# Moving the token-order copies, the SyncE order and the storing of results in a fused attention and MLP kernel

## The chip, the cores and the metric

The kernel runs on one core of a Trainium2 chip. The metric is the device time of one execution in microseconds (us). A core has five engines with instruction streams of their own: TensorE (PE in the profile; its weight loads are PEld), VectorE (DVE), ScalarE (ACT), GpSimd (POOL) and SyncE (SP). SyncE and GpSimd also issue the DMA transfers here; all transfers share the core's 16 DMA engines. An engine takes its instructions in order, and so do the two issuers: an instruction that waits holds up all that stand behind it.

## The reference

There are two stages. The first is attention over 8 batch rows (B), 8 heads (H), 576 positions (S) and a head size (D) of 64. Heads 0 to 3 are sliding: a query sees itself and the 31 positions before it. Heads 4 to 7 are dilated: a query sees every fourth position among the last 128.

```python
mask_plain = (rel >= 0) & (rel < window)                                     # window = 32
mask_dil = (rel >= 0) & (rel < window * dilation) & (rel % dilation == 0)    # dilation = 4
scores = np.where(masks[None, :, :, :], scale * q @ k.T, -1e9)
attn = np.exp(scores - max); attn = attn / (attn.sum(-1) + 1e-9)
x = (attn @ v).transpose(0, 2, 1, 3).reshape(B * S, H * D)                   # 4608 x 512
h = x @ w_in; r = np.maximum(h, 0.0); out = (r * r) @ w_out                  # 512 -> 2048 -> 512
```

(The middle lines are shortened; the meaning is that of the reference.) The second stage is a two-layer network with a squared ReLU between the layers. Inputs and output are fp32.

## The kernel before

**Tiling.** The attention works on one batch row (576 tokens) at a time; the network works on nine chunks of 512 tokens. While PE computes the attention of row b it also computes chunk b-1. The chunk is a Python generator that yields after every few matmuls; `pump(n)` takes n such steps. The attention's program calls `pump` between its own pieces, and so the order of PE's instructions is written out by hand: there is no planner (`tc.manual_schedule()`). Rows 2 to 7 are in a loop at the end of the function; rows 0 and 1 stand in front of it.

**A row.** `attn_scores` computes the scores of the sliding heads (`s_sliding`, tile ps) and of the dilated heads (`s_dilated`, tile pz). ACT takes the exponential into AT, and DVE multiplies AT by the mask. `attn_values` or, from row 4, `attn_values_by_dma` multiplies by the values (`av_sliding`, tile pav, three times with index mp; `av_dilated`, tile paw, four times). DVE normalizes each (`normalize`: a reciprocal and a multiplication, lines 594 and 599). ps, pz, pav and paw share one pool of two PSUM buffers (tag "pa"), so a buffer is free only once DVE or ACT has read it. Then x is transposed into xT, the input of the network: by PE (tiles px and py, copied by ACT) in rows 0 to 3, by DMA transposes in rows 4 to 7 (`x_sliding_by_dma` straight into xT; `x_dilated_by_dma` into yd, from which ACT copies, `x_from`).

**What a row needs of the next one.** q and k have to be transposed into QKTp (sliding) and QKTd (dilated). For rows 2 to 7 this goes through DRAM:

- sliding: GpSimd loads q and k into SBUF (`load_sliding_qk`, tile ns), an engine copies them into token order (`by_token`, line 120, tile nr; DVE, but GpSimd for row 2), SyncE stores them to DRAM (`keep_sliding_qk`, tile dp, line 217), and SyncE transposes them from there (`transpose_sliding`, line 225);
- dilated: GpSimd copies from DRAM to DRAM (`keep_dilated_qk`, tile dd), and SyncE transposes (`transpose_dilated`, line 229).

The values v are loaded by SyncE (sv and sd, lines 132 and 137) and cast by GpSimd into vp and vd. Each block of values also needs a "halo", the end of the block before it on other partitions: ACT copies it in rows 0 and 1 (`halo_sliding`, `halo_dilated`, lines 184 and 189), SyncE copies it by DMA in rows 2 to 7 (lines 194 and 197).

**Order on GpSimd.** `after_transposes(b)` is a tiny GpSimd copy that reads the row's last transposed tile. GpSimd waits there until the transposes have landed, and asks for the next row's q and k only then.

**The copy's place.** In the loop the copy (`turn`) is called from `attn_scores`, hook 3: behind the last dilated scores, in front of the first `normalize` of the values. On DVE it stands there in the program.

**The network.** `mm1_gen` computes one chunk's h (tile ph); ACT applies the ReLU (rt), DVE squares (g). Chunks 0 and 1 use an ordinary second layer (tile po, `store` copies to tile ot and issues a DMA for each 128 tokens). Chunks 2 to 8 use one level of Strassen's scheme (`mm2_strassen_gen`, tiles pa, pb, pc), whose DVE sums gs and g come at the end of mm1. Its results are ou and ov, 512 KB each, and SyncE issues their stores (`leave`) as soon as they are done. ot, ou and ov share a pool of three buffers (`otp`).

## Time and profile before

| | us |
|---|---|
| median of 8 runs | 310.32 (307.46 to 311.36) |
| the profiled execution | 311.36 |
| its span in the trace | 309.1 |

| engine | busy us | share of the span |
|---|---|---|
| PE | 288.3 | 93% |
| DVE | 209.0 | 68% |
| PEld | 192.9 | 62% |
| ACT | 170.8 | 55% |
| POOL | 67.2 | 22% |

The granted clock of TensorE was 1.0. The kernel moved 47.25 MB by DMA, 153 GB/s on the mean; in the slices from about 8 to 230 us the DMA engines are mostly 70 to 100% busy, after that hardly. PE starts at 5.2 us and has short tasks up to 26 us; row 1 runs from about 40 us, row 2 from 62, row 3 from 97, row 4 from 129, row 5 from 161, row 6 from 192 and row 7 from 222 us; chunks 7 and 8 alone take 252.6 to 304.7 us.

How to read it: a row of the timeline gives the start and the length in us, the engine, the line of the kernel, the operation and its tiles, the number of instructions merged into it and, in brackets, how long the engine had been idle before and what released it. Rows of SPq and of DMA operations give the time of issuing, not of the transfer; the landing comes some us later.

### The profile page before, as it was taken

The page shows a single profiled execution, that of the slowest core. Times are in us where ns is not written, and L with a number is a line of the kernel's source. Part 1 is how long each engine was busy: PE and PEld are TensorE (multiplying, and loading weights), DVE is VectorE, ACT ScalarE, POOL GpSimd, SP SyncE. Part 2 cuts the span into 40 slices and gives each one's busy share as a digit, 9 for nine tenths or more (in the row PEclk, how much of TensorE's full clock was granted, in tenths as well). Part 3 has the DMA queues.
Part 4 walks back from the last instruction along what each step waited for, and adds up shares of the span by engine and source line. Part 5 has one row for each costly group of instructions (what it writes and reads, how often), then busy time and mean ns, then how long its engine had stood idle before and what let it go on. Part 6 is the DMA issues. An engine that isn't in the chain of part 4 may idle for free.

```text
span 309.1 us, 6889 instructions
## 1 busy us (share of the span) xinstructions
PE 288.3 (93%) x2762; PEld 192.9 (62%) x2762; DVE 209.0 (68%) x433; ACT 170.8 (55%) x288; POOL 67.2 (22%) x117
## 2 busy tenths in 40 slices
PE   0998998999899999997999999989999999999994
PEld 0644554554455558753898998548855875785583
DVE  7685448668953698477948893989389934834652
ACT  1765648667525863494349535953496446425620
POOL 4381008412805301330035003500240000000000
PEclk9999999999999999999999999999999999999999
DMA  7799996899899999998979998999862130003004
GB/s 113 160 207 215 206 192 109 171 224 219 131 214 210 215 184 196 172 233 187 163 157 257 206 161 159 258 204 154 161 182 40 27 116 33 2 1 138 0 0 138
DMA packets 77521, 47.25 MB, mean 153 GB/s; under 512 B 58545, under 2 KB 69297, under 8 KB 77489
## 3 DMA queue, kind: packets, MB, share of 16 engines
q1 hardware_dynamic: 68416, 32.13, 49.7%
q0 software_dynamic: 9072, 14.68, 27.1%
q8 instruction: 21, 0.34, 0.5%
q14 instruction: 12, 0.09, 0.1%
HBM read 36.70 MB, written 16.52 MB: 172 GB/s over the span
## 4 chain that ended last, share of the span: by engine, by line
PE 68%; DMA 18%; DVE 4%; SPq 3%; POOL 2%; ACT 2%; issue 2%; POOLq 0%
PE ph L299 25%; PE pa L376 15%; DMA ns<-in_q_dram 9%; PE po L442 8%; PE pb L376 7%; DMA QKTd<-dd 4%; PE pc L376 4%; PE paw L627 3%; DMA sv<-in_v_dram 2%; DMA vd<-vd 2%; PE pf L496 2%; PE pav L611 2%; DMA vp<-vp 1%; SPq L229 1%; SPq L225 1%
## 5 line engine op out<-in xcount | busy, mean ns | idle before, releaser
L299 PE MATMUL ph<-xT,wi 128*128 128x512 f16 (+1 forms) x640 | 134.0, 359 | 0.7 <-ACT xT L664 0.7
L322 ACT ACTIVATE rt<-ph 128x512 f16<-128x512 f32 x144 | 86.2, 611 | 48.6 <-PE ph L299 41.2
L299 PEld LDWEIGHTS <-wi 128*128 128x128 f16 x640 | 68.2, 114 | 46.1 <-issue 0.6
L323 DVE TENSOR_TENSOR g<-rt 128x512 f16<-128x512 f16 x144 | 62.8, 448 | 36.9 <-ACT rt L322 36.0
L376 PEld LDWEIGHTS <-g 128*128 128x128 f16 x448 | 43.3, 98 | 6.1
L376 PEld LDWEIGHTS <-gs 128*128 128x128 f16 x336 | 31.9, 98 | 4.4 <-DVE gs L333 0.8
L442 PE MATMUL po<-wo,g 128*128 128x512 f16 x128 | 33.1, 379 | 0.0
L403 DVE TENSOR_TENSOR ov<-pb,ov 128x512 f32<-128x512 f32 x14 | 9.7, 692 | 30.7 <-PE pb L376 17.3
L376 PE MATMUL pa<-wt,gs 128*128 128x256 f16 x224 | 27.5, 273 | 0.0
L376 PE MATMUL pb<-wt,g 128*128 128x256 f16 x224 | 27.1, 273 | 0.0
L169 POOL CAST vp<-sv 128x512 f16<-128x512 f32 x24 | 14.4, 630 | 51.8 <-DMA sv<-in_v_dram 51.8
L177 POOL CAST vd<-sd 128x512 f16<-128x512 f32 (+1 forms) x32 | 22.5, 731 | 9.7 <-PE ps L562 5.4
L392 ACT COPY ov<-pa 128x512 f32<-128x512 f32 x14 | 8.2, 586 | 27.0 <-PE pa L376 27.0
L553 DVE TENSOR_TENSOR AT<-AT,maskp 128x576 f16<-128x576 f16 x32 | 19.2, 619 | 5.1 <-ACT AT L552 4.0
L599 DVE TENSOR_TENSOR xd<-paw,rcp_d 80x512 f16<-80x512 f32 (+1 forms) x32 | 21.9, 684 | 1.1
L552 ACT ACTIVATE AT<-pz 128x576 f16<-128x576 f32 x32 | 19.9, 707 | 1.9 <-PE pz L581 1.8
L552 ACT ACTIVATE AT<-ps 128x576 f16<-128x576 f32 x32 | 19.2, 659 | 1.6 <-PE ps L562 1.1
L611 PEld LDWEIGHTS <-AT 128*128 128x128 f16 x192 | 9.2, 99 | 12.9 <-issue 8.6
L599 DVE TENSOR_TENSOR xs<-pav,rcp_p 96x512 f16<-96x512 f32 x24 | 16.5, 686 | 0.8
L392 ACT COPY ou<-pa 128x512 f32<-128x512 f32 x14 | 8.2, 586 | 15.6 <-PE pa L376 15.6
L611 PE MATMUL pav<-vp,AT 128*128 128x65 f16 x192 | 10.5, 195 | 6.2 <-DVE xs L599 4.2
L553 DVE TENSOR_TENSOR AT<-AT,maskd 128x576 f16<-128x576 f16 x32 | 14.9, 496 | 1.2 <-ACT AT L552 0.4
(83 smaller groups left out, 279.5 us busy)
## 6 DMA issues: line engine op xcount, KB each, us to landing
sv<-in_v_dram SPq DMA_DIRECT2D x14, 288.0 KB, 5.6
dp<-nr SPq DMA_DIRECT2D x12, 288.0 KB, 4.1
out_dram<-ou SPq DMA_DIRECT2D x6, 512.0 KB, 4.0
out_dram<-ov SPq DMA_DIRECT2D x6, 512.0 KB, 4.9
sd<-in_v_dram SPq DMA_DIRECT2D x8, 320.0 KB, 5.8
ns<-in_k_dram POOLq DMA_DIRECT2D x8, 288.0 KB, 7.1
ns<-in_q_dram POOLq DMA_DIRECT2D x8, 288.0 KB, 8.1
sd<-in_v_dram SPq DMA_DIRECT2D x8, 256.0 KB, 6.3
```

The costliest lines, as they stand in the source:

```text
L169: nc.gpsimd.tensor_copy(vp[b % 2][:, m : m + 2, :, 0:D], sv[:, :, m : m + 2, :].rearrange("p h m d -> p m h d"))
L177: nc.gpsimd.tensor_copy(vd[b % 2][p0:P, t, c : c + 2, :, 0:D], sd[p0:P, t, :, D * c : D * (c + 2)].rearrange("p h (c d) -> p c h d", d=D),)
L299: nc.tensor.matmul(ph[:, t0:t1], wi4[ffc // 4][:, dmk, :, ffc % 4], xT[:, dmk, x0 : x0 + t1 - t0], start=(dmk == 0 and t0 == 0), stop=(dmk ...
L322: nc.scalar.activation(rt, ph[:], ACTF.Relu)
L323: nc.vector.tensor_mul(g[:, ffc, :], rt, rt)
L376: nc.tensor.matmul(banks[bank][:, t], a(k, t), b(k), start=(new and t == 0 and k == 0), stop=(k == HF - 1), skip_group_check=True,)
L392: nc.scalar.copy(ot, banks[A])
L442: nc.tensor.matmul(po, g[:, ffc, t * P : (t + 1) * P], wo[ffc // 4][:, ffc % 4, :], start=(ffc == 0), stop=(ffc == NFF - 1),)
L552: nc.scalar.activation(AT[:, u, 0:UW], ps[:, :, 0 : UW // 2], ACTF.Exp, scale=scale)
L553: nc.vector.tensor_mul(AT[:, u, 0:UW], AT[:, u, 0:UW], mask)
L599: nc.vector.tensor_tensor(out=x, in0=pv, in1=rb, op=ALU.mult)
L611: nc.tensor.matmul(pav[:, i, h * (D + 2) : h * (D + 2) + D + 1], AT[:, 2 * (h // 2) + m // 3, off : off + P], vp[b % 2][:, m, h, 0 : D + 1 ...
```

## The change

The change reorders work; matmuls, transfers of q, k and v, and the arithmetic stay.

1. The token-order copy of row 2 moves from GpSimd to DVE, and into row 1's values, behind the first dilated ones. For rows 3, 4 and 5 it moves from hook 3 of the scores to behind the second sliding values (mp == 1). For rows 6 and 7 it stays at hook 3.
2. `leave_half` can hold a store: it is put into the list `held`, and `leave_held()` issues it later. Held are the second half of chunks 0 and 1 and all of chunks 2 to 4. They are issued in the next row right behind the stores of the token-order copy (chunk 0's: behind row 2's transposes). Chunks 0 and 1 are stored by SyncE in two DMAs of 512 KB each, where there were four of 256 KB, chunk 0's by GpSimd.
3. Row 2's q and k are asked for before `cast_dilated_v(1)`. Its sliding transposes stand in front of the dilated ones, and `after_transposes(2)` reads QKTd like that of the other rows.
4. On SyncE, in rows 2 and 3: copy stores, held results, sv, sliding transposes, the dilated transpose of k, the vp halo, the dilated transpose of q, sd. From row 4 on: copy stores, held results, sliding transposes, sv, x, dilated x, dilated transposes, the vp halo, sd.
5. Row 2's halos are made by ACT. Row 1's first ACT halo goes behind its second sliding scores. The loop is split in two (rows 2 and 3, rows 4 to 7), with pumps of 22 and 14 instead of 24 and 16, and a gap of 4 instead of 3 in row 3's scores.

```diff
-        (nc.gpsimd if b == 2 else nc.vector).tensor_copy(
+        nc.vector.tensor_copy(
...
     def after_transposes(b):
-        t = QKTp[b % 2][:, 0, 1, PADP : PADP + 1] if b == 2 else QKTd[b % 2][:, 0, 1, KPAD : KPAD + 1]
-        nc.gpsimd.tensor_copy(seen, t)
+        nc.gpsimd.tensor_copy(seen, QKTd[b % 2][:, 0, 1, KPAD : KPAD + 1])
...
+    held = []
+    def leave_half(c, i, o, m, hold):
+        def go():
+            t0 = c * TOKC + HTOK * i
+            nc.sync.dma_start(
+                out=out[t0 : t0 + HTOK, m].rearrange("(t p) m -> p t m", p=P), in_=o[:, :, m]
+            )
+        if hold:
+            held.append(go)
+        else:
+            go()
+    def leave_held():
+        while held:
+            held.pop(0)()
...
         def leave(o, i, js):
+            leave_half(c, i, o, slice(HM * js[0], HM * (js[-1] + 1)), 1 < c < 5)
...
-        (nc.sync if c else nc.gpsimd).dma_start(out=out[(c * 4 + t) * P : (c * 4 + t + 1) * P, :], in_=ot)
+        if t % 2:
+            leave_half(c, t // 2, halves[c], slice(0, DM), t > 1)
...
+    ns = load_sliding_qk(2)
     cast_dilated_v(1)
-    ns = load_sliding_qk(2)
     dd = keep_dilated_qk(2)
-    nr = by_token(2, ns)
...
-    attn_scores(1, 2, 1)
-    attn_values(1, 1, True)
+    attn_scores(1, 2, 1, {1: lambda: halo_sliding(1, 0)})
+    dp = []
+    attn_values(1, 1, True, lambda: dp.append(keep_sliding_qk(2, by_token(2, ns))))
     pump(1000)
-    dp = keep_sliding_qk(2, nr)
+    transpose_sliding(2, dp[0])
     transpose_dilated(2, dd)
-    transpose_sliding(2, dp)
+    leave_held()
     load_v(2)
...
+        def turn_and_load():                       # rows 2 and 3, behind av_sliding mp == 1
+            dp = turn(nxt, ns)
+            leave_held()
+            load_sliding_v(nxt)
+            transpose_sliding(nxt, dp)
+            cast_sliding_v(nxt)
+            transpose_dilated(nxt, dd, (1,))
+            halo_sliding_by_dma(nxt)
+            transpose_dilated(nxt, dd, (0,))
+            load_dilated_v(nxt, nc.sync)
+        pump(22 if b == 2 else 14)
+        attn_scores(b, 4)
+        attn_values(b, b, False, turn_and_load)
...
+        def copied():                              # rows 4 to 6
+            if nxt < B:
+                dp = turn(nxt, ns)
+                leave_held()
+                transpose_sliding(nxt, dp)
+                load_sliding_v(nxt)
+        def loaded(y):
+            if nxt < B:
+                nc.gpsimd.tensor_copy(seen, y[:, 0, 0, 0:1])
+                cast_sliding_v(nxt)
+                transpose_dilated(nxt, dd)
+                halo_sliding_by_dma(nxt)
+                load_dilated_v(nxt, nc.sync)
+        pump(3)
+        attn_scores(b, 3, 0, {3: copied} if b > 4 else {})
+        attn_values_by_dma(b, copied if b == 4 else None, loaded)
```

(The two comments are added here; `turn` stores the copy that `by_token` makes.)

## The prediction, made before the result was known

> **What bounds the kernel now.** I read the page's busy shares and slices first (PE 288.3 of 309.1 us, granted clock full throughout), then PE in order of time, keeping every row with idle time in front, then DVE at those moments, then what SyncE and GpSimd had issued before.

> PE in order of time, the rows after 50 us that have idle time in front of them (start, length, what, then idle and releaser):

> ```profile
> 51.27 0.31 PE L581 MATMUL pz<-QKTd 64*128 64x80 f16 x8 [0.24 <-ACT AT L552]
> ...
> 52.78 0.29 PE L611 MATMUL pav<-vp,AT 128*128 128x65 f16 x4 [0.54 <-ACT vp L184]
> ...
> 73.23 0.43 PE L562 MATMUL ps<-QKTp 64*128 64x96 f16 x12 [0.60 <-DMA QKTp<-dp]
> ...
> 83.54 0.29 PE L611 MATMUL pav<-vp,AT 128*128 128x65 f16 x4 [1.30 <-DMA vp<-vp]
> ...
> 114.69 0.41 PE L611 MATMUL pav<-vp,AT 128*128 128x65 f16 x8 [0.57 <-DVE xs L599]
> ...
> 142.62 0.41 PE L611 MATMUL pav<-vp,AT 128*128 128x65 f16 x8 [2.19 <-DVE xs L599]
> ...
> 173.24 0.41 PE L611 MATMUL pav<-vp,AT 128*128 128x65 f16 x8 [0.48 <-DVE xs L599]
> ...
> 204.28 0.41 PE L611 MATMUL pav<-vp,AT 128*128 128x65 f16 x8 [1.00 <-DVE xs L599]
> ```

> These eight sum to 6.92 us: 0.78 in row 1, 1.90 in row 2, 0.57, 2.19, 0.48 and 1.00 in rows 3 to 6. From 26 us to 304.7 PE has no other hole, so 6.9 us is all that a reordering can win. The same moments on DVE:

> ```profile
> 140.54 0.76 DVE L120 COPY nr<-ns 128x2304 f16<-128x2304 f16 x1 [2.67 <-DMA ns<-in_q_dram]
> ...
> 171.17 0.76 DVE L120 COPY nr<-ns 128x2304 f16<-128x2304 f16 x1 [1.06 <-DMA vd<-vd]
> ...
> 202.20 0.76 DVE L120 COPY nr<-ns 128x2304 f16<-128x2304 f16 x1 [1.39 <-DMA ns<-in_q_dram]
> ```

> DVE takes its work in order. The copy waits for the next row's q and k, and the normalization of the first sliding values behind it cannot release its bank of two; the third values (pav) stop PE. ("vd" is a mis-attribution: ns of row 6 landed at 171.1.) Why ns is late stands with SyncE and GpSimd:

> ```profile
> 160.76 0.52 SPq L398 DMA_DIRECT2D out_dram<-ou  x1
> 161.89 0.39 SPq L398 DMA_DIRECT2D out_dram<-ov  x1
> ...
> 161.48 0.66 POOL L112 DMA_DIRECT2D ns<-in_k_dram  x1 [0.38 <-issue]
> 162.13 0.62 POOL L112 DMA_DIRECT2D ns<-in_q_dram  x1
> ```

> One MB of results leaves in the same microsecond as the request. The two ns loads take 7.4 and 9.0 us to land there, 7.3 and 9.4 at 192, 7.0 and 7.8 at 132, but 4.2 and 5.7 at 50, where no result leaves.

> [...]

> **The change, part by part.** No matmul is added or removed; I cost each hole.

> *Row 1.* The first halo copy (0.4 us on ACT) goes from behind the dilated scores to before them. The 0.54 hole goes. ACT had 0.27 us of idle there, so about 0.15 comes back in front of pz. I take -0.4; bounds 0 and -0.78.

> *Row 2's q and k, asked for 2.7 us sooner.* They pass four vd casts (2.75 us), which aren't needed until the halo and values some 3 us later: hidden. ns follows w_out on its queue (landing 52.5), so I put its landing at 55 to 56.5, against 57.0. The copy goes from GpSimd (2.10 us) to DVE (0.76), behind the first dilated values, about 57: stores at 57.6, not 59.3. If ns came after 57, each us would delay row 1's last transposes one for one; the margin is about 0.5 us.

> *Row 2's start.* The sliding transposes go ahead of the dilated ones. Pairs of transposes here land about 4 us apart, stores are 1.7 us sooner, but the first result (0.5 MB) is now in front. I expect QKTp at 67 to 68, against 73.1; PE asks at about 71 (pump of 22, not 24, takes off 0.87). Hole 0.60: gone. GpSimd's touch of `seen` now waits for QKTd, about 71, near the old 73.1, so the request for row 3 isn't later.

> *Row 2's halo.* It becomes five ACT copies (3 x 0.45 + 2 x 0.61 = 2.6 us) instead of two DMAs, one of which landed 4.2 us after issue. They fall where ACT is 35% busy (80 to 90 us): hidden, and the 1.30 hole goes. Cover gone if sv lands after 78; I expect 75 to 76.

> *Row 3.* The copy goes behind the second normalization, but gaps of 4 and a pump of 14 (not 3 and 16) put the values one g later, among the Strassen sums. Measured durations from g15 on: 0.42 + 0.69 + 0.69 + 1.22 + 0.20 + 0.69, in the trace 3.76 us from 115.63 to 119.39. Counted from the first pav: g15 can start at +1.97 (its ph ends at +1.30, ReLU 0.60), so the second values are normalized at +5.7; PE reaches the transpose px that reads them at +0.41 + 0.87 + 0.44 + 0.41 + 1.31 + 0.41 + 0.87 + 0.44 = +5.2. A new hole of 0.6 replaces 0.57: net 0, bounds -0.57 and +0.6.

> *Row 4's start.* By the same account row 3's copy ends at 115.9, 2.8 us later than its 113.0, with PE 2.3 us ahead. Its stores land at 119.5 and 120.9 (3.5 and 4.4 us, as now). Behind them: one held result, two sv, two transposes, at 1.4 to 1.6 us each (two sv, two sd and two transposes took 9.8 us there now): QKTp at 127.9 to 128.9, where PE wants it at 127.9. I take +0.5; bounds 0 and +1.2.

> *Row 4.* The copy behind the second values at 139.5, ns by about 136: the 2.19 hole goes. The copy's own 0.76 is covered by the mm1 steps before px would need it (here x goes by DMA).

> *Rows 5 and 6.* The copy stays in front of the first values. With chunks 3 and 4 held, 1 MB doesn't compete: at 1.25 us per 0.5 MB in the mixed stream I take 2.5 us off ns. Row 4's chain adds about 0.8 (below). DVE waits 1.06 and 1.39 now, so both end: -0.4 and -0.9, bounds 0 and -1.48 together.

> *Where the held MB goes.* Behind the stores, in front of QKTp, sv, x and dilated x. Row 4 from the first pav: copy +3.8, stores land +8.4, results +10.9, QKTp +13.3, sv +15.7, x +18.1, dilated x +20. The next chunk's matmuls want x at +21.7 (161.1 less 139.4, the hole taken out). Now x lands at +12. So the late x is hidden with 2 to 3 us to spare. The last dilated-x transpose is released by DVE at +15.2 both before and after; therefore QKTd is issued on time, landing about 0.8 late. The output buffers (three) are free by then: the fourth use needs its result out at about +11, when it has landed at +9.6, and PE has another product to do.

> Sum: -0.4 - 0.6 - 1.3 + 0 + 0.5 - 2.2 - 0.4 - 0.9 = **-5.3 us**. The profiled execution took 311.36 us (span 309.1 and 2.3 around it), so 306.1 for one like it; the runs' median is 310.32, so **305.0**.

> **Rivals.** (1) *Half is given back:* the second normalization among the Strassen sums (row 3) and the late stores (row 4's start) cost their upper bounds, and ns of rows 5 and 6 stays late. -5.3 + 0.6 + 0.7 + 1.3 = -2.7: 307.6. DVE's 97% at 110 to 120 us speaks for it, SyncE's spare time against it. (2) *Nothing moves:* DMA engines are the true bound (share near 1 from 20 to 230 us) and every hole returns elsewhere: 310.3. Against it: row 4's hole ends with the arrival of one load, and after 222 us DMA idles, so what is late is order, not volume. (3) *Slower, by x:* if each held result lands in its crowded 8.2 us (161.89) and not in 1.25 more, results of rows 4 to 6 land at +13.7, QKTp, sv and x take 7.6 more and dilated x 1.8, its copy 0.7: +23.8 against +21.7. That stops PE 2.1 us in three rows, 6.3 against 5.3: 311.3; it decides from a landing 3.6 us beyond mine, and grows to 312.5 if the late `seen` also delays ns by the same 2 us once. For it: those 8.2 us; against: results alone land in 2.8 (251 and 277 us), and the copy now comes when ns and dd have landed. (4) *The copy of row 2 stops DVE in row 1:* ns at 59 would cost 2: 307.

> **How the numbers follow.** Forecast 0.66 (own range 303.4 to 306.9), rival 1 with 4 0.18, rival 2 0.07, rival 3 0.09. Half a per cent, 1.55 us, is about what a measurement of this kernel can tell from no change. Faster: 0.66 and most of rival 1, 0.83; same 0.08; slower 0.09. Low end: all 6.9 us won and half a us of scatter, 302.9. High end, so that rivals 2 and 3 stay outside: 308.4.

> **What would show it.** Right: no idle before pav in rows 4 to 6; nr without a DMA wait; ns landing in 5 to 7 us after its request; the row-2 holes gone; the idle that is left before px in row 3 and before ps at row 4's start, 0.6 and 0.5. Wrong: PE idle before ph at a chunk's first matmul with releaser x or a copy out of yd; before ps with QKTp in rows 3 to 6; a DVE wait on ns in row 1 or 2; ACT waiting for an output buffer in Strassen.

## The result, and the profile after

The changed kernel takes **321.29 us** (median of 11 runs, 319.34 to 323.91) against 310.32 (32 runs, 307.46 to 314.22): a ratio of 1.037, with a 95% interval of 1.033 to 1.040. The prediction was 305.0, in a range of 302.9 to 308.4. It was wrong in its sign. Some executions of a kernel, before's too, are over 1.5% slower than its fastest; the ratios in this document leave them out on both sides.

The profiled execution of after took 322.91 us, with a span of 320.0, 10.9 more than before. PE was busy for 294.3 us (288.3 before) with the same 2762 matmuls, and had 25.7 us of other time (20.8 before). So 4.9 us are new idle time, and 6.0 us are the same matmuls going slower: the mean granted clock was 0.971, not 1.0. PE in order of time, after, the rows past 52 us with over 0.25 us of idle time in front of them:

```profile
54.70 0.41 PE L625 MATMUL pav<-vp,AT 128*128 128x65 f16 x8 [0.42 <-DVE rcp_p L608]
...
117.17 0.26 PE L654 MATMUL px<-ident,xs 96*128 96x96 f16 x2 [1.77 <-DVE xs L613]
...
130.60 0.43 PE L576 MATMUL ps<-QKTp 64*128 64x96 f16 x12 [0.61 <-DMA QKTp<-dp]
...
150.35 1.49 PE L393 MATMUL pa<-wt,gs 128*128 128x256 f16 x12 [0.37 <-DVE gs L350]
160.77 3.57 PE L393 MATMUL pa<-wo,gs 128*128 128x256 f16 x16 [4.57 <-ACT ov L409]
...
195.11 2.84 PE L393 MATMUL pa<-wo,gs 128*128 128x256 f16 x16 [2.10 <-ACT ov L409]
...
228.82 2.44 PE L393 MATMUL pa<-wo,gs 128*128 128x256 f16 x16 [2.10 <-ACT ov L409]
```

Both holes of row 2 are gone, and all four in front of pav in rows 3 to 6. With 0.23 us at 51.87, the holes that are not at "pa<-wo,gs" come to 3.40 us, where all holes of before were 6.92: that part of the change saves 3.5 us. But three new stops of 4.57, 2.10 and 2.10 us stand in the middle of the Strassen layers of chunks 3, 4 and 5. PE waits there for its bank A, which ACT has to empty into ov.

What ACT was doing is in its waits (total, times, longest, in us), after and then before:

```profile
ACT xT L678 <- DMA yd<-xd: 15.8, 4, 6.5
```

```profile
ACT xT L664 <- DMA yd<-xd: 5.6, 5, 1.8
```

ACT stands longer in front of its copy out of yd, the landed dilated x. ACT in order of time in row 4, after and then before:

```profile
151.87 0.59 ACT L409 COPY ov<-pa 128x512 f32<-128x512 f32 x1 [2.83 <-PE pa L393]
158.98 1.26 ACT L678 COPY xT<-yd 128x640 f16<-128x640 f16 x1 [6.52 <-DMA yd<-xd]
160.15 0.57 ACT L409 COPY ov<-pa 128x512 f32<-128x512 f32 x1
```

```profile
153.31 0.59 ACT L392 COPY ov<-pa 128x512 f32<-128x512 f32 x1 [2.39 <-PE pa L376]
154.84 1.29 ACT L664 COPY xT<-yd 128x640 f16<-128x640 f16 x1 [0.94 <-DMA yd<-xd]
156.80 0.59 ACT L392 COPY ov<-pa 128x512 f32<-128x512 f32 x1 [0.67 <-PE pa L376]
```

This is the point that the prediction didn't see. In the program `x_from(b, 0, ...)` stands six pump steps after the last transposes, and there it falls **ahead of Strassen's second copy into ov** (`take(lower, 1)`). ACT took the two copies in the program's order in both traces (at 154.84 and 156.80 us before, at 158.98 and 160.15 after). In before the copy out of yd was through in time: ACT had another 0.67 us of idle time in front of the ov copy. In after the copy out of yd waits for its transfer until 158.95, the ov copy behind it starts only at 160.15, and PE, which wanted the bank at 156.20, starts at 160.77.

Why yd is late is seen on SyncE's queue, after and then before:

```profile
142.57 1.42 SPq L217 DMA_DIRECT2D dp<-nr  x2
144.10 0.52 SPq L297 DMA_DIRECT2D out_dram<-ou  x1
144.67 1.50 SPq L297 DMA_DIRECT2D out_dram<-ov  x1
146.29 5.17 SPq L225 DMA_TRANSPOSE QKTp<-dp  x2
151.51 1.21 SPq L132 DMA_DIRECT2D sv<-in_v_dram  x2
152.76 3.28 SPq L683 DMA_TRANSPOSE xT<-xs  x2
156.14 2.54 SPq L690 DMA_TRANSPOSE yd<-xd  x2
```

```profile
141.33 1.15 SPq L217 DMA_DIRECT2D dp<-nr  x2
142.53 2.29 SPq L132 DMA_DIRECT2D sv<-in_v_dram  x2
145.17 3.09 SPq L669 DMA_TRANSPOSE xT<-xs  x2
148.37 3.49 SPq L225 DMA_TRANSPOSE QKTp<-dp  x2
151.91 3.83 SPq L676 DMA_TRANSPOSE yd<-xd  x2
```

DVE had the first half of dilated x ready at 148.2 us. SyncE takes it 8 us later, because stores, 1 MB of results, QKTp, sv and x are issued first. In before the first of the two yd transposes was issued at 151.91 and landed at 154.81. Stores, sv, x and QKTp stood in front of it there too: what the new order changes among sv, x and QKTp makes little difference to dilated x, which follows all three. What is new in front is the 1 MB (2.2 us, from 144.10 to 146.29); besides, the stores go out 1.2 us later, and QKTp takes 5.17 us to issue and not 3.49.

Each of the three stops is followed by a drop of the granted clock. Stretches of after around the first (us, PE busy, weight loads, DVE, ACT, POOL, granted clock, DMA share, GB/s):

```profile
156.00:158.00 2.00, 0.20 (x2) 0.03 (x1) 0.00 (x0) 0.00 (x0) 0.00 (x0) 1.00 1.09 161
158.00:160.00 2.00, 0.00 (x0) 0.00 (x0) 0.00 (x0) 1.02 (x1) 0.00 (x0) 0.59 0.56 98
160.00:162.00 2.00, 1.23 (x6) 0.86 (x6) 1.25 (x2) 1.73 (x3) 1.73 (x4) 0.50 0.90 182
162.00:164.00 2.00, 2.00 (x11) 1.44 (x10) 0.04 (x1) 0.00 (x0) 0.25 (x2) 0.50 0.77 155
164.00:166.00 2.00, 2.00 (x15) 1.56 (x14) 0.00 (x0) 0.59 (x1) 1.62 (x4) 0.70 0.89 216
```

The clock is half from 158.4 to 165.2 us here, and for 3.4 us each from 195.9 and 230.0. The 16 matmuls at 160.77 took 3.57 us, where such a group takes 1.91 at full clock. As an estimate from these lengths, half clock costs at most half of the busy time in it: 2.2 + 1.7 + 1.7 = 5.6 us. (A fourth such period, from 25.2 us, has nothing to do with these stops; with it the profiled execution is at 0.971, the others of after at 0.973 to 0.988.) The chunks tell the same: chunk 3's second layer starts 1.9 us earlier than before, the matmuls of chunk 4 start 5.4 us later, those of chunk 5 8.7, those of chunk 6 11.3, and it stays so to the end.

### The profile page after: what moved, and what is told of

The parts are those of the page before. It is cut to its first block, busy times and chain, and to the rows that moved or that the text cites. A ratio compares the mean times of both kernels' runs of the same rounds, so it can differ in the third digit from the quotient of the medians.

```text
span 320.0 us, 6877 instructions
## 1 busy us (share of the span) xinstructions
PE 294.3 (92%) x2762; PEld 195.5 (61%) x2762; DVE 209.2 (65%) x434; ACT 172.5 (54%) x293; POOL 62.9 (20%) x112
## 4 chain that ended last, share of the span: by engine, by line
PE 62%; DVE 22%; DMA 7%; ACT 5%; issue 2%; SPq 1%; POOL 1%; DVEq 0%; POOLq 0%
PE ph L316 28%; PE pa L393 11%; PE po L455 7%; PE pb L393 6%; DVE g L340 4%; DVE AT L567 3%; DVE xd L613 3%; DMA yd<-xd 3%; DVE xs L613 2%; PE pc L393 2%; DMA vd<-vd 2%; DVE gs L349 2%; DVE gs L350 2%; PE paw L641 2%; DVE g L420 1%
## 5 line engine op out<-in xcount | busy, mean ns | idle before, releaser
L316 PE MATMUL ph<-xT,wi 128*128 128x512 f16 (+1 forms) x640 | 135.8, 362 | 0.7 <-ACT xT L678 0.7
L340 DVE TENSOR_TENSOR g<-rt 128x512 f16<-128x512 f16 x144 | 63.6, 452 | 40.6 <-ACT rt L339 39.7
L393 PEld LDWEIGHTS <-g 128*128 128x128 f16 x448 | 44.6, 101 | 7.6
L393 PEld LDWEIGHTS <-gs 128*128 128x128 f16 x336 | 33.6, 102 | 14.8 <-issue 9.3
L393 PE MATMUL pb<-wt,g 128*128 128x256 f16 x224 | 29.5, 288 | 0.0
L393 PE MATMUL pa<-wo,gs 128*128 128x256 f16 x112 | 16.7, 311 | 8.8 <-ACT ov L409 8.8
L177 POOL CAST vd<-sd 128x512 f16<-128x512 f32 (+1 forms) x32 | 22.0, 716 | 10.1 <-PE ph L316 4.7
L409 ACT COPY ov<-pa 128x512 f32<-128x512 f32 x14 | 8.2, 584 | 23.8 <-PE pa L393 23.8
L567 DVE TENSOR_TENSOR AT<-AT,maskp 128x576 f16<-128x576 f16 x32 | 17.7, 576 | 4.1 <-ACT AT L566 3.3
L678 ACT COPY xT<-yd 128x640 f16<-128x640 f16 (+1 forms) x8 | 9.5, 1185 | 15.8 <-DMA yd<-xd 15.8
L567 DVE TENSOR_TENSOR AT<-AT,maskd 128x576 f16<-128x576 f16 x32 | 16.3, 533 | 2.1 <-ACT AT L566 0.8
```

The lines of the kernel that those rows point to most:

```text
L177: nc.gpsimd.tensor_copy(vd[b % 2][p0:P, t, c : c + 2, :, 0:D], sd[p0:P, t, :, D * c : D * (c + 2)].rearrange("p h (c d) -> p c h d", d=D),)
L316: nc.tensor.matmul(ph[:, t0:t1], wi4[ffc // 4][:, dmk, :, ffc % 4], xT[:, dmk, x0 : x0 + t1 - t0], start=(dmk == 0 and t0 == 0), stop=(dmk ...
L340: nc.vector.tensor_mul(g[:, ffc, :], rt, rt)
L393: nc.tensor.matmul(banks[bank][:, t], a(k, t), b(k), start=(new and t == 0 and k == 0), stop=(k == HF - 1), skip_group_check=True,)
L409: nc.scalar.copy(ot, banks[A])
L567: nc.vector.tensor_mul(AT[:, u, 0:UW], AT[:, u, 0:UW], mask)
```

## The experiments

The theory: dilated x is late behind the stores and held results, ACT waits for it ahead of the ov copy, and this alone turns the gain into a loss. Rivals: holding the results costs by itself; row 4's or row 3's new place of the token-order copy is to blame; the SyncE order is to blame without any held result. Ratios are to the kernel before on the same chip.

**e1: x and dilated x first** on SyncE in rows 4 to 6, QKTp and sv behind them.

```diff
         def copied():
-                dp = turn(nxt, ns)
+                dps.append(turn(nxt, ns))
                 leave_held()
-                transpose_sliding(nxt, dp)
-                load_sliding_v(nxt)
         def loaded(y):
             if nxt < B:
                 nc.gpsimd.tensor_copy(seen, y[:, 0, 0, 0:1])
+                load_sliding_v(nxt)
+                transpose_sliding(nxt, dps[0])
```

> The changed kernel, but in rows 4 to 6 SyncE issues x and both dilated x before sv and before the next row's sliding transposes; the held results stay behind the copy's stores. Theory (x stands behind transposes that wait for a landing, so the copy out of yd holds ACT and Strassen stops): yd is issued as soon as DVE has normalized it, the three stops before pa (4.57, 2.10, 2.10) and the halved clock after them go, 306 to 308 us. Rival (the held megabyte itself delays x): yd still lands 2 us or more late, stops of 1 to 2 us remain in each row, 312 to 316 us.

Measured: 318.21 us (ratio 1.029, 1.019 to 1.039). The stops at bank A are gone, as the theory has it, but as much idle time is elsewhere (8.79 us, where the three stops were 8.77); PE of e1:

```profile
162.75 0.43 PE L576 MATMUL ps<-QKTp 64*128 64x96 f16 x12 [1.77 <-DMA QKTp<-dp]
...
174.84 0.41 PE L625 MATMUL pav<-vp,AT 128*128 128x65 f16 x8 [1.71 <-DVE xs L613]
...
195.92 0.43 PE L576 MATMUL ps<-QKTp 64*128 64x96 f16 x12 [1.26 <-DMA QKTp<-dp]
...
207.82 0.41 PE L625 MATMUL pav<-vp,AT 128*128 128x65 f16 x8 [1.60 <-DVE xs L613]
...
230.08 0.43 PE L576 MATMUL ps<-QKTp 64*128 64x96 f16 x12 [2.45 <-DMA QKTp<-dp]
```

Now the next row's scores wait for QKTp, and the next request for ns is late (landing at 172.7). The expected time was missed: with the held results in front, each of the two orders tried misses one of the two deadlines. That no other order meets both is not shown.

**e2: nothing held of chunks 2 to 4.**

```diff
-            leave_half(c, i, o, slice(HM * js[0], HM * (js[-1] + 1)), 1 < c < 5)
+            leave_half(c, i, o, slice(HM * js[0], HM * (js[-1] + 1)), False)
```

> The changed kernel, but the results of chunks 2 to 4 are stored at once, as before. Theory (order on SyncE): the sliding transposes still wait for the stores and x still stands behind them; without the megabyte it lands some 2 us sooner, so row 4 keeps a stop of about 2 us and rows 5 and 6 keep little: 310 to 314 us. Rival (held megabyte): all three stops go, 306 to 308 us, if ns is not late again.

Measured: 316.92 us (1.024, 1.010 to 1.037). The stops at bank A shrink to 2.56 and 2.31 us, and a stop before paw of 1.92 comes in. Some 4 us come back; the rest of the loss doesn't need the held results.

**e3: ACT's copies out of yd later**, behind Strassen's second copy into ov (only one copy into ou still stands behind them); a transfer may then be late without holding up the ov copy.

```diff
-        pump(6)
+        pump(13)
         x_from(b, 0, ys[0])
-        pump(7)
         x_from(b, 1, ys[1])
```

> The changed kernel, but both ACT copies out of yd stand behind the second Strassen copy of ov (after 13 steps, not after 6 and 13); no transfer is moved. Theory (x is late, but PE stops only because the copy stands in front of Strassen's on ACT): no idle before pa in rows 4 to 6, at most 1.5 us before the next chunk's first matmul in row 4, 308 to 310 us. Rival (x is later than the next chunk's start anyway): the stops move to the first ph of chunks 4 to 6, 2 us or more in each, 315 us or more.

Measured: 313.82 us (1.011, 0.995 to 1.027): about two thirds of the loss is gone by moving one ACT copy, though the interval is wide, and no wait for the ov copy is left. The 308 to 310 us of the theory isn't reached, so that copy's place alone doesn't make the whole loss: 1.77 us before px, 0.91 before ps and, in rows 5 and 6, 0.82 and 1.41 before pav remain. What shows that the transfer itself still is too late in row 4 is this row of PE in e3:

```profile
162.38 1.33 PE L316 MATMUL ph<-xT,wi 128*128 128x256 f16 x7 [2.60 <-ACT xT L678]
```

Here the wait stands where the prediction had looked for it, in front of the next chunk's matmul, and only in row 4.

**e4: before, with the results of chunks 2 to 4 held, and nothing else.**

```diff
         def leave(o, i, js):
-            nc.sync.dma_start(
...
+            leave_half(t0, o, m, 1 < c < 5)
...
         def turn():
             kept.append(keep_sliding_qk(nxt, by_token(nxt, ns)))
+            leave_held()
             load_sliding_v(nxt)
```

> The kernel before, with one part of the change: results of chunks 2 to 4 are held and issued behind the next row's copy stores. Theory: ns lands about 2.5 us sooner in rows 4 to 6, the waits before pav (2.19, 0.48, 1.00) mostly go, dilated x is late by less than 1 us: 307 to 308.5 us. Rival (held megabyte delays x): stops before pa of 2 us in each of rows 4 to 6 and a halved clock after them, 313 to 316 us.

Measured: 317.63 us (1.028, 1.016 to 1.040). The rival is right: holding alone costs 2.8%, some 8 to 9 us (5.5 us of new idle time in the trace, and two stretches at half clock). The place is the same as in after; PE of e4:

```profile
158.09 1.91 PE L393 MATMUL pa<-wo,gs 128*128 128x256 f16 x16 [2.32 <-ACT ov L409]
...
190.21 3.47 PE L393 MATMUL pa<-wo,gs 128*128 128x256 f16 x16 [2.03 <-ACT ov L409]
225.11 3.25 PE L393 MATMUL pa<-wo,gs 128*128 128x256 f16 x16 [3.30 <-ACT ov L409]
```

**e5: e4 with the late copies of e3**, and **f3: before with the late copies alone**, as a control.

> The kernel before with the results of chunks 2 to 4 held (as in the run that held alone), and both ACT copies out of yd behind the second Strassen copy of ov. Theory (holding costs only through that copy's place on ACT, where dilated x had hardly any slack): the three stops before pa (2.32, 2.03, 3.30) and the halved clock go, nothing of 1 us or more comes in their place in rows 4 to 6, ns stays early: 3 to 5 us below the kernel before, 306 to 309 us. Rival (the DMA stream is full and each relief returns as another wait): idle of PE after 130 us stays at 6 us or more, 313 us or more.

> The kernel before, with both ACT copies out of yd behind the second Strassen copy of ov and nothing else: the control for the runs with late copies. Theory (before, dilated x landed in time, so the copies' place cost nothing): no difference beyond 1 us, 309 to 311 us. Rival (late copies are a gain of their own): 308 us or less.

Measured: e5 310.18 us (0.999, 0.995 to 1.003), f3 309.90 (0.999, 0.995 to 1.002). The late copies do nothing where yd is in time (f3), and take away the whole cost of holding (e4 to e5). So in the kernel before, the held results hurt only through that copy. A gain of holding, which e5 was also expected to have, isn't there in the median. Its profiled execution, its fastest with 307.93, has 0.71 and 0.39 us before pav and nothing in rows 4 and 6; why the other runs don't follow stays open.

**e6: before, with QKTp and sv ahead of x in rows 4 to 6, nothing held.** (sv stood ahead of x already; QKTp alone moves.)

```diff
         def turn():
             kept.append(keep_sliding_qk(nxt, by_token(nxt, ns)))
+            if b > 3:
+                transpose_sliding(nxt, kept[0])
             load_sliding_v(nxt)
         def turned():
-            if nxt < B:
+            if nxt < B and b < 4:
                 transpose_sliding(nxt, kept[0])
```

> The kernel before; in rows 4 to 6 SyncE issues the next row's sliding transposes and sv ahead of x, nothing is held and no copy is moved. Theory: dilated x lands 2 to 3 us later against PE and Strassen stops about 2 us in rows 4 to 6, some with a halved clock after it, on top of the waits for ns: 314 to 318 us. Rival (order is harmless without the held megabyte): 310 to 312 us.

Measured: 312.20 us (1.012, 1.003 to 1.021), less than expected; stops at bank A of 1.34 and 1.04 us in rows 4 and 5. The order alone makes the same stop, but a small one; the larger ones are in the runs with held results (e4) or with the change's later stores (e2).

**e7: rows 1 and 2 of after, the rest of before**, and **e8: e7 with holding and late copies.**

```diff
-    for b in range(2, 4):
+    for b in range(2, 3):
...
-    for b in range(4, B):
+    for b in range(3, B):
```

(In e7 the second loop has the body of before, with `leave_half(..., False)` for chunks 1 to 4; e8 sets `1 < c < 5`, calls `leave_held()` in `turn` and has the edit of e3.)

> The changed kernel up to and with row 2 (chunk 0's second half held, chunk 1 not), rows 3 to 7 as in the kernel before. Theory (the parts in rows 1 and 2 gain what was forecast): no idle of PE before ps and pav in row 2, row 3's chunk starts 1.5 to 2 us sooner, 308 to 309.5 us. Rival (given back at row 3 or by the loop of transfers from row 4 on): 310 to 312 us.

> The two put together: rows 1 and 2 of the changed kernel, rows 3 to 7 of the kernel before with results held and the copies out of yd late. Theory: the gains add, 304 to 307 us. Rival (the stream of transfers sets the rows' length from row 3 on): no better than the one of holding with late copies, 309 us or more.

Measured: e7 309.07 us (0.997, 0.995 to 1.000), e8 307.09 (0.991, 0.988 to 0.994). In e7 the row-2 holes are gone and chunk 2 starts 2.7 us earlier (0.9 of it at chunk 1's start already), but row 3 stops before pav for 2.42 us (113.79) instead of 0.57: an earlier PE meets ns about where it was. With rows 4 to 6 the stops before pav come to 6.61 us, where they were 4.24, and so what rows 1 and 2 won is handed back. e8, with 1.06 us in row 3 and a stop of 1.67 before ph in row 6, beats before by 0.9%.

**f1: after, row 4's copy at hook 3**, as in rows 5 and 6.

```diff
-        attn_scores(b, 3, 0, {3: copied} if b > 4 else {})
-        attn_values_by_dma(b, copied if b == 4 else None, loaded)
+        attn_scores(b, 3, 0, {3: copied})
+        attn_values_by_dma(b, None, loaded)
```

> The changed kernel, with row 4's token-order copy back at hook 3 of the scores (as rows 5 and 6 have it), so that stores, held results and transposes of row 4 start some 3 to 4 us sooner. Theory: of the stop of 4.57 us before pa in row 4 about 1 us is left and the halved clock after it goes, rows 5 and 6 keep theirs: 315 to 318 us. Rival (the copy's place is not part of it, the stream is late anyway): the stop stays at 3 us or more, 319 us or more.

**f2: after, row 3's pump, gap and copy as before.**

```diff
-        pump(22 if b == 2 else 14)
-        attn_scores(b, 4)
-        attn_values(b, b, False, turn_and_load)
+        pump(22 if b == 2 else 16)
+        attn_scores(b, 4 if b == 2 else 3, 0, {3: turn_and_load} if b == 3 else {})
+        attn_values(b, b, False, turn_and_load if b == 2 else None)
```

> The changed kernel, with row 3's pump of 16, gap of 3 and copy at hook 3 as in the kernel before; the rest is the change's. Theory: the 1.77 us before px in row 3 and the 0.61 before ps at row 4's start go, nothing of 1 us comes in their place: 318 to 320 us. Rival (row 4 sets the time whatever row 3 wins): 320.5 us or more, with a longer stop before pa in row 4.

Measured: f1 318.94 us (1.024, 1.010 to 1.037), f2 319.51 (1.029, 1.021 to 1.037). PE of f1, then of f2:

```profile
143.70 0.55 PE L625 MATMUL pav<-vp,AT 128*128 128x65 f16 x8 [3.04 <-DVE xs L613]
...
160.90 1.91 PE L393 MATMUL pa<-wo,gs 128*128 128x256 f16 x16 [0.65 <-ACT ov L409]
193.11 1.91 PE L393 MATMUL pa<-wo,gs 128*128 128x256 f16 x16 [2.12 <-ACT ov L409]
```

```profile
112.26 0.41 PE L625 MATMUL pav<-vp,AT 128*128 128x65 f16 x8 [1.35 <-DVE xs L613]
...
158.38 1.87 PE L393 MATMUL pa<-wo,gs 128*128 128x256 f16 x8 [5.62 <-ACT ov L409]
```

In f1 row 4's stop falls from 4.57 to 0.65 us, but DVE then waits for ns, which lands at 141.55: the request went out at 134.30, late because row 3's copy, behind its second values, had delayed stores, QKTd and with them the request (f4 below, which has row 3 as before, asks at 128.95). In f2 the px and ps holes of 1.77 and 0.61 are gone, and PE waits the longer at bank A. Each edit alone hands its gain to the next wait.

**f4: after with f1, f2 and e3 together.** Holding and the SyncE order of after stay.

> The changed kernel with three things undone at once: row 4's copy early, row 3 as before, the ACT copies out of yd late; held results and SyncE's order stay. Theory (these three places account for nearly all of the loss): PE idle after 100 us under 3 us in all, 305 to 309 us. Rival (the order with held results in front costs by itself, through x before ph or ns before pav): 5 us or more of idle after 100 us, 311 us or more.

Measured: **305.86 us** (305.73 to 306.36; 0.985, 0.978 to 0.992). It beats both kernels. PE of f4, all rows between 100 and 235 us with over 0.2 us of idle time in front:

```profile
113.76 0.41 PE L625 MATMUL pav<-vp,AT 128*128 128x65 f16 x8 [1.71 <-DVE xs L613]
199.47 0.41 PE L625 MATMUL pav<-vp,AT 128*128 128x65 f16 x8 [0.22 <-DVE xs L613]
```

ACT of f4 in row 4, the ov copy now ahead of the copy out of yd:

```profile
153.42 0.59 ACT L409 COPY ov<-pa 128x512 f32<-128x512 f32 x1 [2.91 <-PE pa L393]
154.55 2.28 ACT L678 COPY xT<-yd 128x640 f16<-128x640 f16 x2 [0.54 <-DMA yd<-xd]
```

ns of row 5 is asked for at 128.95, where f1 asks at 134.30, and lands at 134.58, so row 4's early copy doesn't stop DVE; and yd lands at 154.53, where after's lands at 158.95. Not run: f4 without holding, and any two of the three edits without the third. What holding adds in f4, and how the gain divides among the edits, is open.

## Why the prediction was wrong, step by step

*What bounds the kernel* was read rightly: PE's holes, made by late transfers and engines working in order. The holes that it listed did close, but for the 0.24 us before pz in row 1.

*Row 1* (-0.4): the holes went from 0.78 to 0.65; a small miss inside its bounds. The 0.54 went, but a new wait of 0.42 for DVE came before the third values. *Row 2's start and halo* (-1.9): from the start of chunk 1's matmuls to that of chunk 2's, after gains 1.9 us on before. Right.

*Row 3* (0, at most +0.6): the mechanism was right, its size not. The hole before px was 1.77 us, not 0.6. The second values were normalized 6.7 us after the first pav and not 5.7, because g15 started at +2.9 and not at +1.97: the sum had let it start when ACT was done, but DVE still had two masks, two g and the first values to do. The 0.87 and 0.44 us in the sum are lengths of before's trace: eight matmuls into pa took 0.87 us at 115.10, four into pc 0.44 at 115.98. A count along one engine has to begin with what that engine has left.

*Row 4's start* (+0.5): 0.61 before ps, which is in part luck: QKTp landed at 130.56 and not by 128.9, and PE, held up by row 3's hole, asked for it at 129.99 and not at 127.9. *Row 4* (-2.2) and *rows 5 and 6* (-1.3): all three pav holes gone. ns landed 5.2 and 5.6 us after its request at 134 us, 6.0 and 6.6 at 164, 4.7 and 5.5 at 200, about the 5 to 7 predicted. That holding does this is shown by e4, which only holds: its ns loads of rows 4 to 6 take 4.2 to 6.1 us, those of before 7.0 to 9.4, and PE's stops before pav in these rows are gone. Results aren't the only thing that makes ns slow, though: the loads of before at 73.44 and 74.08, which the prediction doesn't list, took 7.1 and 8.4 us, and no result was issued within 10 us before them. GpSimd's requests of after that answer to the one at 161.48 of before:

```profile
164.44 0.65 POOL L112 DMA_DIRECT2D ns<-in_k_dram  x1 [0.38 <-issue]
...
199.65 0.65 POOL L112 DMA_DIRECT2D ns<-in_k_dram  x1 [0.38 <-issue]
```

These and the q loads behind them had landed by 171.65 and 205.77, and the copies on DVE that need them have no wait:

```profile
175.46 0.75 DVE L120 COPY nr<-ns 128x2304 f16<-128x2304 f16 x1
...
209.31 0.75 DVE L120 COPY nr<-ns 128x2304 f16<-128x2304 f16 x1
```

***Where the held MB goes* is the step that failed**, in the words "the late x is hidden with 2 to 3 us to spare". Even by its own figures 1.7 us were to spare (+21.7 less +20), or 1.0 with the copy of 0.7 that rival 3 counts. It failed in three ways.

First, the deadline. It took the next chunk's matmul (+21.7 us from the first pav) as the first to want dilated x. The first is ACT's copy, and behind it in ACT's order stands the ov copy, which PE awaited at +18.57 (156.20 less 137.63). Going back from there, ov copy 0.6 and yd copy 1.26: yd was due at +16.7. The forecast had dilated x at +20, taken here as its second tile; the first lands 1.2 us ahead of it, so at +18.8, and with the landing exactly as forecast PE would still have stopped for 2.1 us in row 4. A view of before could have told it: the ACT rows above, with the copy out of yd 2 us in front of ov.

Second, the landing. Measured from the first pav of row 4, in the order of issue, which is also that of landing: copy +4.2 (forecast +3.8), stores landed +10.1 (+8.4), results +13.8 (+10.9), QKTp +15.9 (+13.3), sv +19.3 (+15.7), x +20.4 (+18.1), dilated x +21.3 and +22.5 (+20). The stores were 1.7 us late, and the second result landed 2.5 us after the first, not 1.25. That 1.25 was an estimate of the author's that no run shows: in before even a result that moves alone (385 and 389 GB/s from 252.5 to 253.5 us) comes to about 1.35 us for its 512 KB. The lateness is kept down to dilated x, whose first tile is 2.5 us behind the forecast's +18.8: with the 2.1 from the deadline these are row 4's 4.57.

Third, the clock. A stop of PE was priced at its length in every case, rival 3 too, and the half clock behind it at nothing. It cost up to 5.6 us more, beside stops of 8.77 us in all; with the stops at their length alone the loss would have been about half as large.

Rival 3 had the right transfer and a fair stop of 2.1 us in three rows, but put it before ph, with a later deadline, and so gave it 0.09. (Its "3.6 us beyond mine" doesn't follow from its own sum, where results 2.8 us later, +13.7 for +10.9, already cost more than is won. The spare time of SyncE, which rival 1 counts against itself, is in the waits of before: 11.3 us in four waits ahead of dilated-x transposes, the longest 4.8.)

## What to carry to other kernels

For a transfer that gets later, look for its first reader in each engine's own order, and for what stands behind that reader: the deadline can be that of an unrelated instruction, here a PSUM copy that frees TensorE's bank (the stop of 4.57 us in row 4). A copy that reads a late transfer goes behind the copies that free PSUM; that one edit cost nothing here where the transfer was in time (f3, ratio 0.999). Price a TensorE stop higher than its length where half clock can follow it: the three of after were 8.77 us long, and the half clock behind them cost up to 5.6 more. Mend waits along one chain together, since each alone can hand its gain to the next, as f1 and f2 did.

## What the runs showed of the hardware

The length of a stop alone doesn't tell whether half clock follows. Behind stops of 2.56 us in e2, 2.32 in e4 and 2.12 in f1 the 16 matmuls into pa took 1.91 us each time, as at full clock. Behind 2.31 in e2, 2.03 in e4 and another 2.12 in f1 they took 2.83, 3.47 and 3.08. The 2.19 us before pav in before left the clock at 1.0; each 2.10 in after was followed by 0.5.

What fits before and after is where a stop lies. The later three half-clock stretches of after begin at 158.36, 195.91 and 230.04 us, and in the 3.41 us up to these points PE was idle for 2.16, 2.10 and 2.10 us. With the traces cut into pieces of that length, counted from the start of a half-clock stretch, no other piece at full clock between 26 and 295 us has more than 1.77 us of idle time (after, 113.99 to 117.40), and the clock stayed full behind all of them. The 2.19 us of before lie across the border of two pieces at 141.50, with 1.07 us on one side and 1.12 on the other. One piece ahead of 26 us, where PE has short tasks, does not fit: in after the one from 21.83 to 25.24 us had only 1.31 us of idle time and was followed by half clock (the fourth period above), so idle time isn't all that counts. This is read from the two traces; no run moved a stop on purpose to test it.
